# Transposes moved from TensorE to the DMA queue, and copies between ScalarE and VectorE, in a linear-attention and MLP kernel

## The chip, the cores and the metric

The kernel runs on one core of one Trainium2 chip. A core has TensorE (matmuls), VectorE, ScalarE and GpSimd (work element by element), SyncE (here it only issues DMA transfers) and 16 DMA engines. The metric is the device time of one launch in microseconds (us), the median of several launches; lower is better. A profile is taken from one launch more. Its span, first to last instruction, is somewhat shorter than the launch. In profiles PE is TensorE, DVE is VectorE, ACT is ScalarE, POOL is GpSimd, and SP or SPq is SyncE with its DMA queue.

## The reference, cut to what matters

Two parts follow each other: a recurrent attention over 768 steps for 4 batches and 8 heads of width 48, and an MLP with a squared relu on its output.

```python
# r, k, v, w: (4, 8, 768, 48); u: (8, 48); w_in: (384, 2048); w_out: (2048, 384)
for t in range(S):
    cur = np.einsum('bhd,bhe->bhde', u[None] * kt, vt)
    y[:, :, t] = np.einsum('bhd,bhde->bhe', rt, state + cur)
    state = wt[:, :, :, None] * state + np.einsum('bhd,bhe->bhde', kt, vt)
x = y.transpose(0, 2, 1, 3).reshape(3072, 384)
h = x @ w_in
g = s * np.maximum(h, 0.0) ** 2 + b
out = g @ w_out                               # (3072, 384), float32
```

## The kernel before

The 768 steps are cut into 6 chunks of 128, so there are 24 chunk-batches, numbered n = 0 to 23. For each of them the kernel loads w, r, k and v (`load n.0` to `load n.3`), takes logarithms and cumulative sums of w (`ln`, `cum`, `exp`, and from n = 8 on `inc` and `exn`), scales r and k with them (`mul`, tile `prd`), transposes both (`tr` with its copy `tev`), multiplies them (`mt`), masks (`msk`), forms the output y (`ymm`, `yev`, tile `x_sb`), transposes that (`xtr` with its copy `xev`) into `xT`, and updates the state (`dmm`, `sup`, `st`). Two chunk-batches make one MLP tile T of 256 tokens. Each of the 12 MLP tiles has eight pieces of the first product (`g1T.i`, 6 matmuls each), their relu (`reluT.i`) and square (`sqT.i`), and eight pieces of the second (`g2T.i`, 4 matmuls each; tile 11 has 12, eight of them of half width), then `oev` and `store`. `li`/`ci` and `lo`/`co` load and cast the four parts of the two weights.

The transposes come in two forms, chosen by the number of the chunk-batch:

```python
def xbar_rk(n):
    return n >= DTK or (n >= DK2 and n % 2 == 1)     # DTK = 9
def xbar_x(n):
    return n >= DTX or (n >= DX2 and n % 2 == 1)     # DTX = 24: never

def trans(n):                       # "tr" on TensorE: 8 matmuls into PSUM
    for x in range(2):
        for p in range(HP):
            nc.tensor.matmul(ps[:, x * HP + p, :], lhsT=..., rhs=identity, is_transpose=True, ...)
def tevac(n):                       # "tev" on ScalarE: PSUM to SBUF
    nc.scalar.copy(out=RK, in_=c["trps"])
def dtrans(n):                      # "tev" as one transposing DMA instead of both
    nc.sync.dma_start_transpose(out=RK, in_=c["prd"].rearrange("t x h d -> t (x h d)"))

def xtr(n):                         # "xtr" on TensorE: 3 matmuls into PSUM
    for i in range(KT):
        nc.tensor.matmul(ps[:, i, :], lhsT=c["x"][:, i*128:(i+1)*128], rhs=identity, is_transpose=True, ...)
def xevac(n):                       # "xev" on ScalarE
    nc.scalar.copy(out=xT[T][:, :, j * L : (j + 1) * L], in_=c["xt_ps"])
def dxtr(n):                        # "xev" as one transposing DMA
    nc.sync.dma_start_transpose(out=xT[T][:, :, j * L : (j + 1) * L], in_=cb[n]["x"])
```

The MLP, with two PSUM buffers for `h_ps`:

```python
def g1(T, i):
    ps = psH.tile([128, FPQ, TOK], FP32, name="h_ps", tag="h")        # 2 buffers
    for f in range(FPQ):              # 2
        for kt in range(KT):          # 3
            nc.tensor.matmul(ps[:, f, :], lhsT=w_in_sb..., rhs=xT[T][:, kt, :], ...)
def relu(T, i):
    rh = mlp.tile([128, FPQ, TOK], BF16, name="rh", tag="rh", bufs=4)
    nc.scalar.activation(out=rh, in_=hs[T, i], func=AF.Relu)
def square(T, i):                     # on ScalarE or VectorE, by the order's text
    ...
def warm(n):                          # n matmuls on zeros, into a tile that nobody reads
    for _ in range(n):
        nc.tensor.matmul(warm_ps, lhsT=warm_sb[:, 0:128], rhs=warm_sb, start=True, stop=True)
```

The order in which instructions are issued isn't left to a scheduler. It is a text of words that an earlier search found, and each engine runs its own words in that order. A word such as `g10.4` is piece 4 of `g1` of MLP tile 0; `+5` is a call of `warm(5)`; a suffix `@A` or `@D` puts the word on ScalarE or VectorE in place of its default engine.

Of the kernel before, what the change touches and what calls it, by code (L numbers as in the profile page):

```python
# [24 lines left out]
PK = 2  # L25
PKD = 1.55
ONE = 8
DTK = 9
DTX = 24
DK2 = 24  # L30
DX2 = 24
SQE = 'DA'
# [15 lines left out]
g11.3 load6.0 colsum1 rkp4 g20.1 ln5 relu1.2 tr4 rku4 relu1.3 load4.3 cum5 sq1.0@A g11.4 st1 exp5
g11.5 co2 g20.5 tev4 load5.1 sq1.3 load5.2 colsum2 sq1.1@A st3 co3 mt4 load7.0 relu1.4 g20.6
relu1.5 cd4 g11.6 load6.1 msk4 sq1.5@A colsum3 ln6 g20.7 yd4 sq1.4@A load6.2 cssplit g11.7 sq1.2@A  # L50
l25 l24 vb4@A csspread load5.3 cum6 csevac g20.2 mul5 exp6 load8.0 dmm4 g20.3 rkp5 sup4 ln7
load6.3 tr5 oev0.0 ymm4 rku5 tev5 cum7 load7.1 yev4 g21.0 oev0.1 exp7 l26 xtr4 mul6 load7.2 g21.1
xev4 mt5 relu1.6 cd5 vb5 load7.3 g21.4 relu1.7 st2 msk5 yd5 dmm5 g21.2 ln8 load9.0 sq1.7@A st4
sup5 tr6 cum8 vb6 store0.1 tev6 ymm5 rkp6 g21.5 yev5 exp8 load8.1 g21.6 inc8 l27 sq1.6@A dmm6 xtr5
mul7 g21.7 load8.3 xev5 exn8 mt6 rkp7 sup6 vb7@A load8.2 g12.0 msk6 load9.1 g12.1 rku7 ln9 tr7
oev1.1 relu2.0 load10.0 rku6 cum9 relu2.1 cd7 dmm7 g12.2 inc9 tev7 l28 load11.0 g12.3 cd6 st5
relu2.2 ymm6 yd6 sup7 load9.2 exp9 g12.4 relu2.3 sq2.0 mt7 yd7 yev6 exn9 load9.3 g12.5 relu2.4
msk7 st7 g21.3 sq2.2@A store0.0 sq2.1 rkp8 g12.6 oev1.0 sq2.3 load10.1 ymm7 relu2.6 st6 xtr6 g22.4
yev7 ln10 load10.2 mul8 relu2.5 g22.0 ln11 xtr7 sq2.4 load12.0 g22.5 xev6 sq2.6@A load10.3 cum10
# [24 lines left out]
inc19 exp19 load19.1 g16.7 mul18 load19.2 g17.0 relu6.7 tev16 g26.1 exn19 ln20 dmm16 g26.5 vb18@A
sup16 load19.3 sq6.7 cum20 g17.1 vb17 inc20 relu7.0 tev17 g26.6 rkp18 sq6.6@A dmm17 relu7.1 g17.2
st16 exp20 load20.1 dmm18 g26.7 sq7.0@A mul19 exn20 g26.2 tev18 relu7.2 rkp17 oev6.1 g17.3 sup17
mt16 rku17 relu7.3 load20.2 g17.4 msk16 sq7.3 g26.3 yd16 relu7.4 load21.0 g17.5 sup18 sq7.2@A vb19
cd17 sq7.1 ymm16 rku18 tev19 oev6.0 mt17 relu7.5 g27.0 msk17 l219 yd17 g27.4 st17 load21.1 g17.6
yev16 ymm17 st18 load21.2 xtr16 mt18 yev17 xev16 g27.5 sq7.5@D relu7.6 load22.0 sq7.4 xtr17 cd18
g17.7 xev17 mul20 ln21 g27.1 relu7.7 dmm19 load20.3 yd18 msk18 g18.0 sq7.7 sq7.6@A g27.2 rkp19  # L90
store5.1 sup19 relu8.0 g27.6 rku19 mt19 tev20 g18.1 msk19 rkp21 ymm18 relu8.1 g18.2 load23.0 sq8.0
g27.3 store6.1 rku21 cd19 relu8.2 load22.1 cum21 ln22 g18.3 sq8.1@D exp21 ymm19 yd19 inc21 relu8.3
g18.4 oev7.0 sq8.2@A rkp20 g27.7 load22.2 yev19 relu8.4 yev18 g18.5 sq8.3 rku20 oev7.1 load23.1
mt20 relu8.5 load21.3 xtr18 xtr19 msk20 vb20@A g18.6 xev18 g28.0 load22.3 relu8.6 supn20 sq8.5@D
g18.7 sq8.4 xev19 store6.0 exn21 cum22 g19.0 relu8.7 inc22 rkp22 ln23 g28.1 load23.2 relu9.0 g28.4
mul21 sq8.6@A store7.0 g19.1 exp22 supn21 cd20 exn22 g28.5 tev21 yd20 relu9.1 cum23 ymm20 exp23
g19.2 yev20 g28.6 inc23 relu9.2 mul22 g19.3 sq8.7 exn23 g28.2 tev22 sq9.1 mul23 g19.4 sq9.2@A
xtr20 relu9.3 cd21 g28.3 load23.3 sq9.0 sq9.3 g28.7 yd21 oev8.0 relu9.4 store7.1 g19.5 store8.0
rku22 mt21 relu9.5 g19.6 vb22 msk21 sq9.5 st19 g29.4 vb21@A tev23 xev20 g19.7 oev8.1 relu9.6
supn22 cd22 ymm21 sq9.4@A g29.5 yd22 yev21 relu9.7 mt22 sq9.6@A vb23 g29.0 sq9.7@D xtr21 rkp23  # L100
msk22 g29.6 xev21 g29.1 rku23 g110.0 ymm22 relu10.0 g110.1 yev22 mt23 cd23 relu10.1 g110.2 yd23
msk23 xtr22 g29.7 relu10.2 supn23 sq10.0@A g110.3 xev22 ymm23 relu10.3 g110.4 yev23 g29.2 sq10.1@D
relu10.4 g110.5 sq10.3 sq10.4 oev9.1 xtr23 g110.6 relu10.5 sq10.2 xev23 g210.0 sq10.5@D relu10.6
g110.7 g111.0 relu10.7 g210.1 relu11.0 g111.1 g210.2 relu11.1 g111.2 sq11.0@A sq10.6@A g29.3
sq10.7 g111.3 oev9.0 relu11.2 g210.3 sq11.1@D relu11.3 store9.0 store8.1 g111.4 sq11.2@A g210.4
relu11.4 g111.5 g210.5 relu11.5 g111.6 sq11.5@D oev10.0 g210.6 relu11.6 sq11.3@D store10.0 g111.7
store9.1 g211.0 relu11.7 g210.7 sq11.4@A sq11.7@D sq11.6@A g211.1 oev10.1 g211.4 store10.1 g211.2
g211.8 g211.5 g211.3 g211.6 oev11.0 g211.9 g211.7 store11.0 g211.10 oev11.1 g211.11 store11.1
oev11.2 store11.2
"""  # L110

class Plan:

# [43 lines left out]
def kernel(  # L160
# [550 lines left out]
        T, j = divmod(n, CPT)  # L711
        if j == 0:
            xT[T] = mlp.tile([128, KT, TOK], BF16, name="xT", tag="xT", bufs=XTB)
        nc.scalar.copy(out=xT[T][:, :, j * L : (j + 1) * L], in_=c["xt_ps"])  # L714


    def load_win(i):
# [40 lines left out]

    def relu(T, i):
        rh = mlp.tile([128, FPQ, TOK], BF16, name="rh", tag="rh", bufs=4)  # L760
        nc.scalar.activation(out=rh, in_=hs[T, i], func=AF.Relu)  # L761
        hs[T, i] = rh

    def sq_eng(T, i):
# [385 lines left out]
```

## Time and profile before

| what | before |
|---|---|
| device time, median of 3 (lowest to highest) | 187.79 us (187.76 to 187.91) |
| span of the profile | 186.2 us |
| TensorE: busy, matmuls | 180.6 us, 1994 |
| VectorE busy | 131.5 us |
| ScalarE busy | 142.4 us |
| GpSimd busy | 103.8 us |
| transposing DMAs, median time to landing | 15, 3.3 us |
| mean granted TensorE clock | 0.999 of full speed |

Busy time counts a matmul from its start to its modelled end. Matmuls overlap, so the busy time can exceed the time they take from the queue: where this document speaks of a **slot** it means the time from the start of one group of matmuls to the start of the next group on TensorE. The chain of waits is followed back from the last instruction, each step to what released it. The timeline lists instructions in order of time.

### The profile page before, as it was taken

How to read it: one execution, taken by the hardware profiler on the slowest of the kernel's cores; microseconds unless marked ns; L12 is line 12 of the kernel's file. 1: busy time of each engine (PE TensorE's matmuls, PEld its weight loads, DVE VectorE, ACT ScalarE, POOL GpSimd, SP SyncE). 2: the span in 40 equal slices, each digit the busy share in tenths (PEclk: the TensorE clock that was granted, in tenths of full speed). 3: DMA queues.
4: the chain of work that ended last, by engine and by line, in shares of the span. 5: the costliest groups of instructions: out<-in, count | busy, mean ns of one | idle time of the engine just before them, and what ended most of it. 6: DMA issues, size and time to landing. Idle time of an engine off the chain costs nothing.

```text
span 186.2 us, 5073 instructions
## 1 busy us (share of the span) xinstructions
PE 180.6 (97%) x1994; PEld 142.3 (76%) x1994; DVE 131.5 (71%) x220; ACT 142.4 (76%) x277; POOL 103.8 (56%) x141
## 2 busy tenths in 40 slices
PE   7999999999999999999999999999999999999992
PEld 5667888866678788687778877877787877887871
DVE  7478888556799768986987878658788577452231
ACT  3576798797979999769798779974689886678530
POOL 3787840608798695949956265695892167100000
PEclk9999999999999999999999999999999999999999
DMA  6998999888989999999488989999698272000322
GB/s 161 264 308 239 331 318 280 295 180 177 207 190 229 197 221 240 187 213 188 118 199 171 246 164 252 194 186 208 146 212 211 59 184 59 2 0 4 112 99 86
DMA packets 117610, 34.14 MB, mean 183 GB/s; under 512 B 112338, under 2 KB 115539, under 8 KB 117587
## 3 DMA queue, kind: packets, MB, share of 16 engines
q1 hardware_dynamic: 117586, 33.83, 78.3%
q8 instruction: 15, 0.25, 0.5%
q14 instruction: 9, 0.07, 0.1%
HBM read 25.17 MB, written 4.72 MB: 160 GB/s over the span
## 4 chain that ended last, share of the span: by engine, by line
PE 74%; SPq 12%; DMA 7%; DVE 4%; issue 1%; DVEq 0%
PE o_ps L792 31%; PE h_ps L748 29%; SPq L297 8%; DMA wi_st<-in_moe_w_in_dram 5%; PE mt_ps L543 3%; DMA rkt<-in_k_dram 2%; PE y_ps L606 2%; PE xt_ps L699 2%; PE y_ps L597 2%; PE cums L388 2%; PE d_ps L638 1%; DVE gT L773 1%; SPq L719 1%; SPq L305 1%; PE trps L477 1%; SPq L729 1%
## 5 line engine op out<-in xcount | busy, mean ns | idle before, releaser
L748 PE MATMUL h_ps<-xT,w_in 128*128 128x256 bf16 x576 | 77.6, 273 | 0.1
L792 PE MATMUL o_ps<-w_out,gT 128*128 128x384 bf16 (+1 forms) x400 | 75.3, 320 | 0.0
L761 ACT ACTIVATE rh<-h_ps 128x512 bf16<-128x512 f32 x96 | 56.5, 598 | 14.5 <-PE h_ps L748 13.5
L748 PEld LDWEIGHTS <-w_in 128*128 128x128 bf16 x576 | 60.6, 114 | 6.7 <-POOL w_in L880 0.2
L792 PEld LDWEIGHTS <-gT 128*128 128x128 bf16 x400 | 36.2, 98 | 15.3
L771 ACT ACTIVATE gT<-rh 128x512 bf16<-128x512 bf16 x62 | 37.2, 629 | 0.3
L352 POOL TENSOR_TENSOR yd<-vt,cd 128x384 bf16<-128x384 f32 x22 | 20.1, 919 | 30.4 <-DVE cd L346 18.3
L554 DVE TENSOR_TENSOR mt_sb<-mt_ps,tri_strict 128x1024 bf16<-128x1024 f32 x22 | 26.8, 1219 | 4.2 <-PE mt_ps L543 3.8
L323 POOL TENSOR_TENSOR rkp<-rkt 128x384 f32<-128x384 f32 x22 | 24.5, 1112 | 4.7 <-DMA rkt<-in_k_dram 4.6
L329 POOL TENSOR_TENSOR rku<-rkp,u_bc 128x384 f32<-128x384 f32 x24 | 26.0, 1087 | 0.9
L451 DVE TENSOR_TENSOR prd<-rkt,E 128x768 bf16<-128x768 f32 x22 | 23.0, 1045 | 2.8 <-DMA rkt<-in_k_dram 1.6
L803 DVE SCALAR_TENSOR_TENSOR o_sb<-o_ps,s_bc,bconst 128x384 f32<-128x384 f32 (+1 forms) x25 | 14.9, 596 | 10.3 <-PE o_ps L792 10.0
L651 DVE TENSOR_TENSOR x_sb<-y_ps,yd 128x384 bf16<-128x384 f32 x24 | 13.2, 554 | 11.3 <-PE y_ps L606 10.4
L773 DVE TENSOR_TENSOR gT<-rh 128x512 bf16<-128x512 bf16 x34 | 15.8, 482 | 4.9 <-ACT rh L761 4.9
L714 ACT COPY xT<-xt_ps 128x384 bf16<-128x384 bf16 x24 | 11.5, 478 | 6.8 <-PE xt_ps L699 6.8
L346 DVE TENSOR_REDUCE cd<-rku 128x8 f32<-128x384 f32 x24 | 13.0, 543 | 0.9 <-POOL rku L329 0.9
L688 POOL TENSOR_TENSOR st<-stmp,l 128x384 bf16<-128x384 bf16 x16 | 13.1, 829 | 0.7 <-DVE stmp L679 0.7
L1109 PE MATMUL warm_ps<-warm_sb 128*128 128x256 bf16 x74 | 12.2, 309 | 1.1 <-DVE warm_sb L1066 1.1
L424 DVE TENSOR_TENSOR inc<-cums,logw 128x384 f32<-128x384 f32 x16 | 8.9, 554 | 5.5 <-ACT rh L761 1.6
L318 ACT ACTIVATE logw<-wt 128x384 bf16<-128x384 f32 x22 | 11.5, 522 | 1.5 <-DMA wt<-in_w_dram 1.3
L880 POOL CAST vb<-vt 128x384 bf16<-128x384 f32 x14 | 7.4, 536 | 7.6 <-DMA vt<-in_v_dram 4.9
L464 POOL TENSOR_TENSOR l<-E,par 128x8 f32<-128x8 f32 x20 | 7.0, 353 | 6.6 <-ACT E L419 4.7
(96 smaller groups left out, 198.1 us busy)
## 6 DMA issues: line engine op xcount, KB each, us to landing
out_dram<-o_sb SPq DMA_DIRECT2D x23, 192.0 KB, 2.8
wt<-in_w_dram SPq DMA_DIRECT2D x22, 192.0 KB, 3.9
rkt<-in_r_dram SPq DMA_DIRECT2D x22, 192.0 KB, 4.0
rkt<-in_k_dram SPq DMA_DIRECT2D x22, 192.0 KB, 3.8
vt<-in_v_dram SPq DMA_DIRECT2D x22, 192.0 KB, 3.7
wi_st<-in_moe_w_in_dram SPq DMA_DIRECT2D x4, 768.0 KB, 7.5
wo_st<-in_moe_w_out_dram SPq DMA_DIRECT2D x4, 768.0 KB, 7.6
pkt<-in_w_dram SPq DMA_DIRECT2D x1, 384.0 KB, 3.3
```

The costliest lines, as they stand in the source:

```text
L297: nc.sync.dma_start(out=dst, in_=src[bb, :, t0 : t0 + L, :].transpose([1, 0, 2]))
L323: nc.gpsimd.tensor_tensor(out=rkp, in0=c["r"], in1=c["k"], op=ALU.mult)
L329: nc.gpsimd.tensor_tensor(out=rku.rearrange("t h d -> t (h d)"), in0=c["rkp"].rearrange("t h d -> t (h d)"), in1=u_bc, op=ALU.mult,)
L352: nc.gpsimd.tensor_tensor(out=yd, in0=c["v"], in1=c["cd"].unsqueeze(2).to_broadcast([128, H, D]), op=ALU.mult,)
L451: nc.vector.tensor_tensor(out=prd[:, :, :, 0:D], in0=c["rk"], in1=c["E"][:, :, 0:HD].rearrange("t x (h d) -> t x h d", h=H), op=ALU.mult,)
L554: nc.vector.tensor_tensor(out=m.rearrange("s g p t -> s (g p) t"), in0=c["mt_ps"].rearrange("s g p t -> s (g p) t"), in1=(masks[n % 2] if ...
L748: nc.tensor.matmul(ps[:, f, :], lhsT=w_in_sb[ft // FPP][:, kt, :].rearrange("p (m j) -> p j m", j=FPP)[:, ft % FPP, :], rhs=xT[T][:, kt, : ...
L761: nc.scalar.activation(out=rh, in_=hs[T, i], func=AF.Relu)
L771: nc.scalar.activation(out=g, in_=rh, func=AF.Square)
L773: nc.vector.tensor_tensor(out=g, in0=rh, in1=rh, op=ALU.mult)
L792: nc.tensor.matmul(os_[T, k][:, cols], lhsT=gT[T][:, ft, tt * 128 : (tt + 1) * 128], rhs=w_out_sb[ft // FPP][:, ft % FPP, cols], start=(ft ...
L803: nc.vector.scalar_tensor_tensor(out=o_sb[:, cols], in0=os_.pop((T, k))[:, cols], scalar=s_bc, in1=bconst[:, cols], op0=ALU.mult, op1=ALU.add,
```

## The change

One chunk-batch more (n = 8) has its r and k transposed by a DMA, and the last four (n = 20 to 23) have x transposed by a DMA; before, no x was. That takes these transposes off TensorE and their copies off ScalarE. The copy of x out of PSUM and the relu can now run on VectorE too, where the order's text says so, which is meant to share the work between ScalarE and VectorE more evenly. The order's text is new from end to end, since it was searched again for the new choices. It has 80 warm-up matmuls where the old one had 74. By its suffixes and defaults the new text puts 26 of 96 relus and 10 of the 20 remaining copies of x on VectorE; the squares on ScalarE go from 62 to 63, the casts of v there from 10 to 11, one cast of `w_out` moves from VectorE to ScalarE, and one cast of `w_in` from VectorE to GpSimd.

```diff
@@ -25,8 +25,8 @@
 PK = 2
 PKD = 1.55
 ONE = 8
-DTK = 9
-DTX = 24
+DTK = 8
+DTX = 20
 DK2 = 24
 DX2 = 24
...
@@ the order of issue @@
 ORDER = """
-load0.0 load0.1 load_u load0.2 load2.0 ln0 ln1 load2.1 +18 cum0 load2.2 u_mm exp0 load0.3 +2 cum1
-l20 mul0 li0 exp1 rkp1 u_ev +1 tr0 load3.1 ln2 mul1 tev0 load3.2 +6 cum2 rku1 +2 tr1 exp2 load2.3
-l21 tev1 mul2 vb0@A l22 cd1 +14 mt0 rkp2 vb1@A msk0 +5 dmm0 load3.0 rkp0 tr2 sup0 +1 mt1 tev2 li1
-rku0 st0 msk1 ci0 load3.3 rku2 cd0 +13 mt2 li2 ymm0 yd0 msk2 vb2@A yd1 +1 ymm1 li3 yev0 rkp3 ln3
-xtr0 yev1 xev0 +3 cum3 cd2 rku3 dmm2 xtr1 exp3 load4.0 sup2 +6 dmm1 xev1 mul3 lo0 ci1@A +2 ymm2
-g10.0 l23 cd3 yd2 sup1 g10.1 relu0.0 vb3 yev2 tr3 relu0.1 small2 yd3 g10.2 tev3 dmm3 ci2@D g10.3
-relu0.2 xtr2 sup3 mt3 sq0.0@A load4.1 g10.4 sq0.1 relu0.3 msk3 ci3 g10.5 relu0.4 lo1 xev2 ymm3 ln4
-sq0.2 relu0.5 g10.6 sq0.3 load4.2 yev3 cum4 relu0.6 load5.0 xtr3 g10.7 co0 xev3 lo2 g11.0 relu0.7
-sq0.4 sq0.5 g20.0 relu1.0 sq0.6 sq0.7 colsum0 exp4 lo3 g11.1 g11.2 co1 relu1.1 small g20.4 mul4
-g11.3 load6.0 colsum1 rkp4 g20.1 ln5 relu1.2 tr4 rku4 relu1.3 load4.3 cum5 sq1.0@A g11.4 st1 exp5
-g11.5 co2 g20.5 tev4 load5.1 sq1.3 load5.2 colsum2 sq1.1@A st3 co3 mt4 load7.0 relu1.4 g20.6
-relu1.5 cd4 g11.6 load6.1 msk4 sq1.5@A colsum3 ln6 g20.7 yd4 sq1.4@A load6.2 cssplit g11.7 sq1.2@A
-l25 l24 vb4@A csspread load5.3 cum6 csevac g20.2 mul5 exp6 load8.0 dmm4 g20.3 rkp5 sup4 ln7
-load6.3 tr5 oev0.0 ymm4 rku5 tev5 cum7 load7.1 yev4 g21.0 oev0.1 exp7 l26 xtr4 mul6 load7.2 g21.1
-xev4 mt5 relu1.6 cd5 vb5 load7.3 g21.4 relu1.7 st2 msk5 yd5 dmm5 g21.2 ln8 load9.0 sq1.7@A st4
-[... cut: 50 lines ...]
-msk22 g29.6 xev21 g29.1 rku23 g110.0 ymm22 relu10.0 g110.1 yev22 mt23 cd23 relu10.1 g110.2 yd23
-msk23 xtr22 g29.7 relu10.2 supn23 sq10.0@A g110.3 xev22 ymm23 relu10.3 g110.4 yev23 g29.2 sq10.1@D
-relu10.4 g110.5 sq10.3 sq10.4 oev9.1 xtr23 g110.6 relu10.5 sq10.2 xev23 g210.0 sq10.5@D relu10.6
-g110.7 g111.0 relu10.7 g210.1 relu11.0 g111.1 g210.2 relu11.1 g111.2 sq11.0@A sq10.6@A g29.3
-sq10.7 g111.3 oev9.0 relu11.2 g210.3 sq11.1@D relu11.3 store9.0 store8.1 g111.4 sq11.2@A g210.4
-relu11.4 g111.5 g210.5 relu11.5 g111.6 sq11.5@D oev10.0 g210.6 relu11.6 sq11.3@D store10.0 g111.7
+load0.0 load_u load0.2 load0.1 load2.0 load2.1 ln0 +18 u_mm ln1 load2.2 +1 cum0 exp0 load0.3 +5
+cum1 mul0 load3.0 rkp0 exp1 +1 tr0 load2.3 ln2 mul1 tev0 li0 +6 cum2 l20 u_ev +2 tr1 exp2 rku0
+load3.1 tev1 mul2 load3.2 vb0@A +15 mt0 vb1 cd0 tr2 ln3 msk0 rkp1 load3.3 dmm0 tev2 l21 sup0 l22
++7 mt1 rku1 st0 dmm1 msk1 li1 yd0 sup1 +10 cum3 rkp2 load4.0 cd1 ymm0 exp3 yd1 lo0 +1 ymm1 ci0
+yev0 l23 rkp3 li2 mt2 yev1 xtr0 mul3 +2 xtr1 xev0 vb2@A rku2 xev1@D vb3@A +7 tr3 li3 msk2 g10.0
+tev3 dmm3 ci1 load5.0 sup3 +5 mt3 relu0.0@D dmm2 g10.1 sup2 rku3 sq0.0@A g10.2 cd2 relu0.1 load4.1
+msk3 ymm2 yd2 relu0.2 g10.3 ln4 co0 sq0.1@A ymm3 load4.2 yev2 g20.0 cd3 xtr2 ci2 g20.4 sq0.2 yd3
+cum4 lo1 yev3 exp4 g10.4 relu0.3@D ci3 xtr3 small2 xev2@D g10.5 sq0.3@A relu0.4@D ln5 colsum0 lo2
+relu0.5@D sq0.4@A g10.6 xev3@D g10.7 lo3 relu0.6 sq0.5 cum5 relu0.7 mul4 g11.0 sq0.6@A g11.1 rkp4
+relu1.0 load4.3 tr4 relu1.1 load6.0 g11.2 co1 tev4 g11.3 sq0.7 load5.1 exp5 g20.1 relu1.2@D
+colsum1 relu1.3 co2 g11.4 sq1.0@A g20.5 l25 rku4 small relu1.4@D g11.5 co3@A load5.2 mt4 cd4 g20.2
+sq1.4 vb4 load7.0 colsum2 yd4 colsum3 g20.6 cssplit ln6 load6.1 msk4 l24 csspread dmm4 load6.2
+g20.7 csevac sq1.1 load5.3 sq1.3@A g11.6 sq1.2@A mul5 cum6 load8.0 relu1.5 g20.3 exp6 rkp5 sup4
+tr5 load6.3 oev0.0 g11.7 ln7 rku5 relu1.6@D tev5 ymm4 load7.1 oev0.1 cum7 relu1.7 g21.4 yev4
+load7.2 exp7 mul6 xtr4 g21.0 load9.0 vb5 st2 cd5 mt5 st4 xev4@D st1 tr6 ln8 st3 msk5 g21.5 load7.3
+rkp6 tev6 dmm5 g21.1 sup5 load8.3 sq1.5@A l26 cum8 yd5 ymm5 inc8 exp8 g21.6 load8.1 rku6 vb6@A
+[... cut: 44 lines ...]
+ln23 g28.0 oev7.1 sq8.4@A tev21 g28.1 inc22 sq8.6@A g28.4 cd20 exn22 xev19@D yd20 cum23 load21.3
+g28.5 inc23 exp23 store7.1 g19.0 supn21 sq8.7@D mt20 rkp22 relu9.0@D load23.2 g28.6 msk20 st18
+g19.1 g19.2 load23.3 mul22 ymm20 relu9.2 g28.2 store6.1 relu9.1 sq9.2 mt21 yev20 tev22 sq9.1 g28.7
+vb21 msk21 sq9.0@A yd21 g19.3 exn23 xev20 g19.4 relu9.3 mul23 g28.3 sq9.3 load22.3 relu9.4 ymm21
+vb23 oev8.0 g19.5 sq9.4@A tev23 st19 yev21 g19.6 oev8.1 relu9.5 rkp23 g29.0 sq9.5 relu9.6@D
+store7.0 g29.1 rku22 supn22 g29.2 sq9.6 xev21 g19.7 rku23 cd22 mt22 relu9.7 g29.4 yd22 store8.0
+msk22 g29.5 vb22 g29.6 sq9.7@D mt23 ymm22 g29.7 yev22 g110.0 cd23 xev22 msk23 yd23 g29.3 relu10.0
+g110.1 sq10.0@A oev9.0 g110.2 relu10.1 supn23 store9.0 ymm23 sq10.1@D relu10.2 g110.3 yev23
+sq10.2@A g210.0 relu10.3@D g110.4 oev9.1 xev23 g110.5 sq10.3@D relu10.4@D g210.4 relu10.5 store8.1
+g210.5 sq10.4@A store9.1 sq10.5@D g210.1 g110.6 g110.7 relu10.6@D g210.2 relu10.7 g111.0 sq10.6@A
+g111.1 relu11.0@D g210.6 sq11.0 relu11.1 sq10.7@D g111.2 sq11.1@D g111.3 relu11.2@D g210.3
+relu11.3 g111.4 sq11.3@D oev10.0 g111.5 relu11.4@D store10.0 g211.0 relu11.5 sq11.2 g111.6 sq11.5
...
@@ -711,7 +712,11 @@
         T, j = divmod(n, CPT)
         if j == 0:
             xT[T] = mlp.tile([128, KT, TOK], BF16, name="xT", tag="xT", bufs=XTB)
-        nc.scalar.copy(out=xT[T][:, :, j * L : (j + 1) * L], in_=c["xt_ps"])
+        out = xT[T][:, :, j * L : (j + 1) * L]
+        if pl.ops["xev", n]["eng"] == "ACT":
+            nc.scalar.copy(out=out, in_=c["xt_ps"])
+        else:
+            nc.vector.tensor_copy(out=out, in_=c["xt_ps"])
 
 
     def load_win(i):
@@ -758,7 +763,10 @@
 
     def relu(T, i):
         rh = mlp.tile([128, FPQ, TOK], BF16, name="rh", tag="rh", bufs=4)
-        nc.scalar.activation(out=rh, in_=hs[T, i], func=AF.Relu)
+        if pl.ops["relu", T, i]["eng"] == "ACT":
+            nc.scalar.activation(out=rh, in_=hs[T, i], func=AF.Relu)
+        else:
+            nc.vector.tensor_scalar_max(out=rh, in0=hs[T, i], scalar1=0.0)
         hs[T, i] = rh
 
     def sq_eng(T, i):
```

## The prediction

> **What bounds the kernel now.** I read the page first (busy times), then the chain of waits in order of time, then busy time by stage, then TensorE's timeline.
>
> The page has TensorE busy all the time:
>
> ```profile
> span 186.2 us, 5073 instructions
> PE 180.6 (97%) x1994; PEld 142.3 (76%) x1994; DVE 131.5 (71%) x220; ACT 142.4 (76%) x277; POOL 103.8 (56%) x141
> L748 PE MATMUL h_ps<-xT,w_in 128*128 128x256 bf16 x576 | 77.6, 273 | 0.1
> L761 ACT ACTIVATE rh<-h_ps 128x512 bf16<-128x512 f32 x96 | 56.5, 598 | 14.5 <-PE h_ps L748 13.5
> ```
>
> The first row after the span is busy time, the next two are groups: busy time, mean ns of one, idle time before them with what ended it. The 97% alone shows little, as one `h_ps` matmul lasts 273 ns but the six of a piece take 0.65 us of the queue, 109 ns each. The chain of waits (start, duration, what) shows where TensorE really sets the pace:
>
> ```profile
> 39.27 4.35 DMA rkt<-in_k_dram
> 43.74 0.97 DVE prd L451
> 44.76 0.62 PE trps L477 x8
> 45.99 0.67 PE o_ps L792 x4
> 63.91 0.45 PE trps L477 x8
> 172.11 0.65 PE h_ps L748 x6
> 176.68 5.90 PE o_ps L792 x52
> 182.60 0.42 DVE o_sb L803
> ```
>
> Up to 44.76 us the chain passes through transfers: the last is the k of chunk-batch 5 (`load5.2`), which releases `mul5` (tile `prd`) and with it the eight transposes `tr5`. After that the chain has only TensorE rows in all its longer steps, until the last matmul ends at 182.6. Is there slack inside these rows? I added up slots, from TensorE's timeline: 0.65 us a `g1` or `g2` piece (0.33 half width), 0.45 a `tr`, 0.165 an `xtr`, 0.33 an `mt`, 0.38 a `ymm` with a state (0.21 without, 0.98 in the packed n = 0, 1), 0.17 a `dmm` (0.45 packed), 0.95, 0.43, 0.26 and 0.16 the four kinds of `cum`, and 0.31, 0.49 and 0.84 for `colsum`, `csspread` and `u_mm`. All that stands behind `tr5` in the order of before comes to 134.8 us. It took 182.6 - 44.8 = 137.8. The 3 us between are mostly rounding of the slots and the change of tile shape after an `mt`; I found no single hole over 0.2 us. Hence **TensorE bounds the kernel from 45 us on, with nearly no wait in it**, and transfers bound the head. Busy time by stage agrees (stretch, its length, then PE, PEld, DVE, ACT, POOL busy, the clock, the DMA share and GB/s):
>
> ```profile
> 22.00:44.70 22.70, 22.02 (x259) 18.04 (x254) 15.59 (x27) 19.30 (x37) 9.03 (x12) 1.00 0.92 259
> 44.70:80.00 35.30, 35.24 (x407) 27.48 (x408) 30.43 (x47) 31.07 (x62) 28.35 (x36) 1.00 1.04 210
> 80.00:120.00 40.00, 40.00 (x435) 32.24 (x434) 31.52 (x50) 35.07 (x73) 25.42 (x35) 1.00 0.92 195
> 120.00:163.00 43.00, 43.00 (x462) 33.90 (x460) 30.66 (x49) 32.53 (x66) 25.39 (x29) 1.00 0.66 141
> 163.00:182.60 19.60, 19.57 (x162) 15.73 (x159) 6.77 (x15) 11.01 (x21) 0.00 (x0) 1.00 0.15 54
> ```
>
> ScalarE is at 88% between 45 and 120 us, close behind but not the bound; the DMA engines are full until 120 and nearly idle at the end.
>
> **What the Trainium skill says.** (1) "Perfetto Trace Analysis", Identifying the Most-Contended Engine: matmul busy time is no measure of how near TensorE is to its limit, since matmuls overlap. The trace agrees (273 ns busy, 109 ns of queue), so I count slots. (2) "VectorE: DVE Perf Modes", The three transpose paths: 390 ns on TensorE and 1309 ns by DMA for one 128x128 block. Here a block costs TensorE only 56 ns of queue (eight in 0.45 us), and eight blocks by DMA land 3.3 us after issue. (3) "ScalarE: Activation LUTs", What ACT_TABLE_LOAD costs: 186 ns + 0.833 ns an element, 612 ns for a relu of 512; the trace has 598. (4) "VectorE: DVE Perf Modes", Why PSUM operands drop a tier: float32 from PSUM runs at one element a cycle, and two at most otherwise. The trace has no single-source float32 op of 512 from PSUM, but two-source ones: 554 ns for 384 elements (`x_sb`) and 1219 for 1024 (`mt_sb`), 1.04 ns an element.
>
> **The change part by part.**
>
> 1. *r and k of n = 8 by DMA.* Removed: `tr8`, eight matmuls, the row at 63.91 us, 0.45 us, in a stretch where TensorE has no hole. Also a copy of 1.01 us on ScalarE. Added: a transposing DMA of some 3.3 us to landing, at about 62 to 65 us, where the DMA share is 1.04. So **-0.45 us**, if `mt8` stands far enough behind. In the new order, where `tev8` is issued just behind `xtr7`, four `g1` and four `g2` pieces, two `cum` and two `dmm` stand between `xtr7` and `mt8`: 8 x 0.65 + 2 x 0.26 + 2 x 0.17 = 6.1 us.
> 2. *x of n = 20 to 23 by DMA.* Removed: 4 x 0.165 = 0.66 us of TensorE and four copies of 0.48 us on ScalarE, between 147 and 165 us. Added: four DMAs where the share is 0.66 falling to 0.15. From `ymm21` to `g110.0` ten pieces of 0.65 us stand in the new order, and ten between `ymm23` and `g111.0`: 6.5 us each, against about 0.55 (`yev`) + 3.3 (landing, as an estimate from the larger transpose). Hidden: **-0.66 us**.
> 3. *Warm-ups.* Six more, at the 0.11 us that one takes in the filled queue: +0.66 us of TensorE, five of them just behind `dmm3` in tile 0's `g1`. They are padding for a wait that the search expected there.
> 4. *Relu and copies of x on VectorE.* Relu on VectorE, estimated from the two rows above: 554 + 128 x 1.04 = 0.69 us, 26 of them 17.9 us; ten copies at 0.35 to 0.55, 3.5 to 5.5; less one square (0.48) and two casts (0.96 each). VectorE goes from 131.5 to about 151 us. ScalarE loses 26 x 0.598 + 14 x 0.478 + 1.01 = 23.2 us and gains a square (0.63), a cast of v (0.51) and one of w_out (1.5, as `w_in`'s 1486 ns): about 122 us. As TensorE had no wait on ScalarE behind 45 us that would show, this frees **nothing by itself**.
> 5. *The new order.* I compared what stands ahead of `tr5`, the first instruction of the saturated part. The loads ahead of `load5.2` are the same set in both orders. TensorE's words ahead of `tr5` are the same too, but for six more warm-ups (+0.66) and `g11.7` moved behind it (-0.65): 38.71 us of slots before, 38.72 after. So `tr5` should start at about 44.8 again. Behind it stand 134.8 + 0.65 - 0.45 - 0.66 = 134.3 us of slots, **0.46 us less**.
>
> Sum: the DMA fixes the head, the removed transposes are worth 1.11 us, the warm-ups eat 0.66 of it. 187.79 - 0.46 = 187.33. As a new order was searched for and kept, I take a little off for holes that it may have closed in the head: **187.2 us**.
>
> **Rivals.** (a) *The head gets faster:* warm-ups in the queue cost nothing if TensorE would have waited anyway, and `tr5` may come earlier, by a better order of transfers. For it: the chain of before passes through the queue of transfers from 15 to 44 us. Against it: the same bytes stand ahead of `load5.2`, and the share is already 0.92. It would give the full 1.1 us or somewhat more: 186.0 to 186.7. (b) *VectorE becomes the bound:* the new text puts ten VectorE relus in tiles 0 to 2, and a late relu holds one of only two `h_ps` buffers. For it: VectorE is at 86% between 45 and 80 us already (30.43 of 35.3). Against it: in tiles 3 to 8 only seven relus move. TensorE would get holes of some tenths each, 1 to 3 us in all: 188 to 190. (c) *The head gets slower:* `load4.0` and `lo0` now stand ahead of `li2`, 0.96 MB at about 260 GB/s, 3.7 us later, and `g10.4` needs it. The new order has `g20.0`, `g20.4` and the warm-ups ahead of `g10.4` to fill that, some 1.9 us. What isn't filled is lost only if it is still there at `tr5`: up to +1 us. (d) *A transposing DMA delays loads* around 65 us by its few us: loads run ahead by several chunk-batches there, so I give it little.
>
> **Range and chances.** (a) sets the low end, (b) and (c) the high end: 186.1 to 188.9. Two per cent are 3.8 us, more than any of the rivals but a bad (b) could make. Faster by over 2%: 0.02, within: 0.94, slower: 0.04.
>
> **What would show it.** TensorE has 1980 matmuls (1994 - 20 + 6); `trps` has 64 and `xt_ps` 60. `tr5` starts near 44.8 us (step 5; earlier speaks for (a), later for (c)). From there to the last matmul it is about 137.4 us (steps 1, 2); more means holes, with `h_ps` matmuls waiting for VectorE (b). ScalarE busy is near 122, VectorE near 151, one relu on VectorE near 0.69 us (step 4). The prediction fails if the new order's holes in the head differ from the old one's by more than a microsecond, which I can't read from an order alone.

## The result, and the profile after

The changed kernel takes **189.92 us** (median of 4 runs, 189.5 to 191.04) against 187.77 us for the kernel before in the same comparison: a ratio of **1.0129, 95% interval 1.0081 to 1.0177**. It is 2.15 us slower where 187.2 us and a small gain were predicted, and it lies above the predicted range.

The profiled execution is the one of 191.04 us, so its times run about 1 us above the median. Its page, with the span, the busy times and the group of the new relus (busy time, mean ns of one | idle time before it and what ended it):

```profile
span 189.1 us, 5050 instructions
PE 182.1 (96%) x1980; PEld 142.2 (75%) x1980; DVE 152.5 (81%) x253; ACT 126.0 (67%) x239; POOL 106.2 (56%) x141
...
L769 DVE TENSOR_SCALAR rh<-h_ps 128x512 bf16<-128x512 f32 x26 | 17.8, 683 | 6.2 <-PE h_ps L753 5.9
```

The balance of work came out as meant: fewer matmuls, ScalarE relieved of 16 us, 21 us more on VectorE. TensorE is still at 96%. Neither row shows a loss. The chain of waits does (start, duration, what):

```profile
22.24 1.38 DVE prd L452
...
28.36 0.58 DVE w_out L890
...
31.76 0.69 DVE rh L769
32.50 0.81 PE h_ps L753 x6
...
46.98 0.72 DVE prd L452
47.75 0.62 PE trps L478 x8
...
54.02 0.57 DVE inc L425
54.67 0.50 ACT E L420
55.21 0.40 PE mt_ps L544 x8
```

Two things differ from before. `tr5`, the row at 47.75 us, is **3.0 us later** (44.76 before). And the chain ahead of it no longer runs through transfers: from 22 to 32 us it runs mostly through VectorE, with the new relu (31.76 us) in it, and from 32.5 us on mostly through TensorE, but for 2.8 us on ScalarE (36.8 to 39.6 us) and the product `prd` just ahead of `tr5`. Behind `tr5` it still leaves TensorE now and then, as at 54.02 us, where `mt` waits for an `exp` behind an `inc` on VectorE. The last matmul ends at 185.9, 138.2 us after `tr5`; it was 137.8 before.

**A ledger of lost time.** With the slots of the prediction I added up TensorE's useful work ahead of a mark, by each kernel's own text and without warm-ups, and took it from the time at which the mark starts. What is left is lost time: waits, warm-ups, and matmuls at a lower rate. Unlike the bare times of marks, it lets orders be compared that have done different work by then. In us:

| stretch | before | after | difference |
|---|---|---|---|
| start, to the first `g1` piece (21.95; 24.12) | 12.44 | 14.54 | +2.10 |
| middle, from there to `tr4` (34.91; 36.57) | 0.67 | 2.06 | +1.39 |
| `tr4` to `tr5` (44.76; 47.75) | 1.08 | 1.23 | +0.15 |
| `tr5` to the last matmul's end (182.56; 185.93) | 3.02 | 3.86 | +0.84 |
| useful work removed | | | -1.11 |
| sum | | | +3.37 |

The text does have 1.11 us less work in it. The changed order adds four times as much lost time, most of it ahead of `tr4`, where the prediction had counted only the warm-ups.

### The profile page after: what moved, and what is told of

It reads as the page before. It is cut to its first block, busy times and chain, and to the rows that moved or that the text cites. A ratio compares the mean times of both kernels' runs of the same rounds, so it can differ in the third digit from the quotient of the medians.

```text
span 189.1 us, 5050 instructions
## 1 busy us (share of the span) xinstructions
PE 182.1 (96%) x1980; PEld 142.2 (75%) x1980; DVE 152.5 (81%) x253; ACT 126.0 (67%) x239; POOL 106.2 (56%) x141
## 4 chain that ended last, share of the span: by engine, by line
PE 80%; DVE 7%; issue 2%; ACT 2%; POOL 1%; DVEq 0%; ACTq 0%
PE h_ps L753 30%; PE o_ps L800 30%; PE mt_ps L544 4%; PE warm_ps L1117 2%; PE y_ps L607 2%; DVE prd L452 2%; PE cums L389 2%; PE y_ps L598 2%; PE trps L478 2%; PE xt_ps L700 2%; PE d_ps L639 1%; DVE rh L769 1%; DVE inc L425 1%; ACT E L420 1%; PE y_ps L587 1%
## 5 line engine op out<-in xcount | busy, mean ns | idle before, releaser
L753 PE MATMUL h_ps<-xT,w_in 128*128 128x256 bf16 x576 | 74.1, 273 | 0.4 <-DVE rh L769 0.2
L767 ACT ACTIVATE rh<-h_ps 128x512 bf16<-128x512 f32 x70 | 41.2, 596 | 25.2 <-PE h_ps L753 24.4
L779 ACT ACTIVATE gT<-rh 128x512 bf16<-128x512 bf16 x63 | 38.1, 627 | 1.6 <-DVE rh L769 1.1
L452 DVE TENSOR_TENSOR prd<-rkt,E 128x768 bf16<-128x768 f32 x22 | 27.8, 1265 | 1.4 <-ACT E L435 0.8
L769 DVE TENSOR_SCALAR rh<-h_ps 128x512 bf16<-128x512 f32 x26 | 17.8, 683 | 6.2 <-PE h_ps L753 5.9
L781 DVE TENSOR_TENSOR gT<-rh 128x512 bf16<-128x512 bf16 x33 | 17.7, 543 | 1.8 <-ACT rh L767 1.7
L652 DVE TENSOR_TENSOR x_sb<-y_ps,yd 128x384 bf16<-128x384 f32 x24 | 13.2, 550 | 4.9 <-PE y_ps L607 2.8
L689 POOL TENSOR_TENSOR st<-stmp,l 128x384 bf16<-128x384 bf16 x16 | 14.1, 884 | 5.4 <-DVE stmp L680 5.4
L1117 PE MATMUL warm_ps<-warm_sb 128*128 128x256 bf16 x80 | 13.4, 316 | 1.1 <-DVE warm_sb L1074 1.1
L420 ACT ACTIVATE E<-cums 128x388 f32<-128x388 f32 (+1 forms) x16 | 7.9, 493 | 8.3 <-DVE inc L425 5.9
L347 DVE TENSOR_REDUCE cd<-rku 128x8 f32<-128x384 f32 x24 | 12.9, 539 | 0.0
L413 ACT ACTIVATE E<-cums 128x768 f32<-128x768 f32 x8 | 6.5, 817 | 8.6 <-PE cums L381 4.7
```

Of the source, the lines that this page charges most:

```text
L452: nc.vector.tensor_tensor(out=prd[:, :, :, 0:D], in0=c["rk"], in1=c["E"][:, :, 0:HD].rearrange("t x (h d) -> t x h d", h=H), op=ALU.mult,)
L753: nc.tensor.matmul(ps[:, f, :], lhsT=w_in_sb[ft // FPP][:, kt, :].rearrange("p (m j) -> p j m", j=FPP)[:, ft % FPP, :], rhs=xT[T][:, kt, : ...
L769: nc.vector.tensor_scalar_max(out=rh, in0=hs[T, i], scalar1=0.0)
L779: nc.scalar.activation(out=g, in_=rh, func=AF.Square)
L781: nc.vector.tensor_tensor(out=g, in0=rh, in1=rh, op=ALU.mult)
```

## The experiments

Theory A blamed one word: `u_mm` (two float32 matmuls of one row for u) now stands ahead of `cum0` and delays the start. Rivals were VectorE as the bound (B), GpSimd holding VectorE up, and the order of transfers or of words as a whole. Below, ratios are to the kernel before, with 95% intervals; medians are over all executions, while ratios leave out those that ran in a slower state of the chip.

**1. `u_mm` back behind `cum0`, in the changed kernel** (`e1_after_u_late`).

```diff
-+18 u_mm ln1 load2.2 +1 cum0 exp0
++18 ln1 load2.2 +1 cum0 u_mm exp0
```

> The changed kernel, with the spread of u (u_mm, two float32 matmuls) issued behind cum0 instead of ahead of it, as in the kernel before. Theory A (u_mm stands ahead of cum0 while TensorE is still cold, and the head of the whole attention chain shifts by it): cum0 starts near 4.9 us instead of 6.8, g10.0 near 22 instead of 24.1, time 187.7 to 188.2, about 2 us less than the changed kernel's 189.9. Rival B (VectorE is the bound, by relus and copies): within 0.4 us of 189.9. Rival C (the transposing DMAs cost it): within 0.4 us of 189.9.

Measured: 190.94 us, 1.0163 [1.0104, 1.0222]. The first `g1` piece does start 1.5 us earlier (22.61 us), but `tr5` only 0.8 (46.98). The waits of TensorE from 20 to 50 us (in all, times, longest) show one that took its place, for the last cast of w_out:

```profile
PE cs_ps L839 <- ACT w_out L886: 1.5, 1, 1.5
PE o_ps L800 <- DVE w_out L890: 0.5, 1, 0.5
...
```

The kernel is no faster than the changed one (189.92 us, 1.0129): in time, the whole of the earlier start is lost again. As the whole cause, A falls.

**2. The same word moved early, in the kernel before** (`e2_before_u_early`): `+18 cum0 load2.2 u_mm` becomes `+18 u_mm cum0 load2.2`.

> The kernel before, with u_mm moved ahead of cum0 and nothing else. Theory A: cum0 starts near 6.7 us, g10.0 near 24, time 189.3 to 190.0, about 2 us more than before's 187.8. Rivals B and C: 187.8, as nothing of VectorE or of the transposes changes.

Measured: 188.98 us, 1.0097 [1.0059, 1.0134]. In an order that is otherwise unchanged the word costs 1.4 us, or 1.8 by the ratio. `cum0` starts at 6.42 us where it was at 4.87. So an early `u_mm` is harmful in this order, and in the changed one taking it away is not enough.

**3. The transposes alone, in the kernel before** (`e3_before_crossbar`): `DTK = 8`, `DTX = 20`, without `tr8` and `xtr20` to `xtr23`.

> The kernel before in its own order, with only the transposes of the change: r and k of n=8 and x of n=20 to 23 by DMA, their TensorE words left out of the order. Theory A, and the step of the prediction that values the removed transposes at 1.11 us: 186.5 to 187.0. Rival C (DMA transposes stall the order): 188 or more, with TensorE holes near 65 us or behind 147 us.

Measured: 186.95 us, 0.9973 [0.9949, 0.9997]. It is a gain, of about half the 1.11 us of slots (the interval reaches from 0.1 to 1.0 us). A wait that may have eaten the rest, from 60 to 75 us:

```profile
PE mt_ps L543 <- DMA RK<-prd: 1.1, 1, 1.1
```

In the old order the transfer has too little in front of `mt8`; the changed order has more, and its `mt8` doesn't wait for the transfer. With `DTX = 20` alone (`e10_before_x_only`):

> The kernel before with only x of n=20 to 23 by DMA; r and k of n=8 stay on TensorE. With both by DMA in before's order, mt8 waited 1.14 us for its transposing DMA, which takes back more than the 0.45 us of tr8. So without that: 0.66 us less than before, 186.7 to 187.0, and not slower than with both.

Measured: 188.23 us, 1.001 [0.9979, 1.0041]: no gain outside the interval, with one wait of 0.4 us for a transposed x. Without the wait of `mt8` it should have been the faster of the two, and it was not. So whether these four are worth their 0.66 us, and whether that wait is what halved the gain of experiment 3, stays open.

**4. All relus and copies of x on ScalarE, in the changed kernel** (`e4_after_scalar`): the `@D` of 26 relus and 10 `xev` is taken off.

> The changed kernel with all 26 relus and 10 copies of x on ScalarE again. Theory A: still 189 to 190.5, as the late head stays; VectorE busy near 131, ScalarE near 145. Rival B (VectorE is what slows it): 187.5 to 188.5, and the mean of the prd products back from 1265 to about 1050 ns.

Measured: 192.71 us, 1.0265 [1.0221, 1.0309]. Sharing with VectorE **helps**, by about 2.5 us (from the two ratios to before). It helps behind `tr5` (140.6 us to the end in place of 138.2), and changes little ahead of it (`tr5` at 47.39 us).

**5. The two orders joined at `tr5`.** `e5_head_before` has the order of before up to `tr5`, then the changed one; `e6_head_after` is its mirror image, with before's transposes. Each word of the second part that the first has issued already is left out.

> The changed kernel with the order of before up to tr5 (74 warm-ups, u_mm behind cum0, all relus and copies of x there on ScalarE) and its own order behind it. tr5 should then start near 44.9 us, as in the kernel before. Theory H (the loss is made in the head, by the order of transfers, the cold TensorE and warm-ups): 187.0 to 187.8, with 137.4 to 138 us from tr5 to the last matmul. Theory S (the stretch from 45 to 75 us, where VectorE and ScalarE hold each other up, makes it too): 188.3 to 189.2, with 139 or more from tr5 to the end.

> The kernel before with the changed order up to tr5 (80 warm-ups, u_mm ahead of cum0, relus and copies of x partly on VectorE), and its own order and transposes behind it. Theory H: tr5 near 47.4 us, 189.7 to 190.7. Theory S: no more than about 188.5, since the new order's stretch behind tr5 is absent.

Measured: 187.51 us, 0.9999 [0.9978, 1.0019], and 191.01 us, 1.021 [1.016, 1.0261]. The loss goes with the head. Yet the first has 1.11 us less work and gains nothing by it, so the changed order behind `tr5` is no better either.

**6. More of the head repaired.** `e7_u_late_loads` is experiment 1 with before's sequence of loads up to `load5.2`. `e9_u_late_wout_early` is experiment 1 with the last three parts of w_out loaded earlier and `co3` on VectorE.

> The changed kernel with u_mm behind cum0 and, on the transfer queue, the loads up to load5.2 in the order of before (li0 two loads earlier, li2 and li3 ahead of load4.0 and lo0). Theory H in its form that the order of transfers sets tr5: tr5 near 45 us, 187.8 to 188.6. If the order of transfers doesn't matter and VectorE's own order in the head does: tr5 near 47, as with u_mm late alone, and about 190.5.

> The changed kernel with three repairs of its head: u_mm behind cum0; lo1 ahead of load4.2 and load5.0, and lo2, lo3 before small2, so that the parts of w_out land earlier; the cast co3 on VectorE (0.96 us) in place of ScalarE (1.48). lo0 stays early. If the head's waits are what is left of the loss once u_mm is late (with u_mm late alone colsum3 waited 1.46 us for that cast, and nothing was gained): no wait of TensorE on w_out over 0.5 us, tr5 near 45.5 us, time 188.0 to 189.0. If something else holds the head: tr5 at 47 or later and 190 or more.

Measured: 191.64 us, 1.0223 [1.0171, 1.0275], and 190.74 us, 1.0181 [1.0142, 1.022]. In `e7` TensorE waits for the first w_out part:

```profile
PE o_ps L799 <- DVE w_out L889: 2.4, 1, 2.4
```

The new words have `g20.0` early and need `lo0` early; before's loads bring it late. Behind that wait TensorE's matmuls ran at half rate for a while, as the last section shows. In `e9` the wait of experiment 1 is gone, and smaller ones stand in its place:

```profile
PE trps L477 <- DVE prd L451: 0.7, 2, 0.6
PE o_ps L799 <- DVE w_out L889: 0.5, 1, 0.5
PE h_ps L752 <- ACT rh L766: 0.4, 1, 0.4
...
```

**7. GpSimd's products on one head of eight**, in both kernels (`e12_after_gpsimd_cut`, `e13_before_gpsimd_cut`). Most of the product of r, k and u is left out, so the outputs differ from the reference.

> The changed kernel, with GpSimd's products r*k and r*k*u on one head of eight only (the rest of the diagonal term is left out, the sum on VectorE reads the same number of elements); so its output isn't the reference's. Theory L (VectorE's products of two float32 tiles in SBUF, tile prd, are held up while GpSimd runs its own): the mean of the prd products falls from 1265 to about 950 ns, mul5 no longer takes 1.75 us, and the time falls by 0.8 to 2 us from 189.9. If the hold-ups lie off the path: prd faster all the same, and the time within 0.5 us.

> The same cut of GpSimd's two products in the kernel before, as the other half of the comparison. The mean of prd falls from 1045 to about 950 ns. Theory L (hold-ups on VectorE make the new order slower): the gain here is small, under 0.4 us, so that the distance of the two kernels shrinks from 2.1 us to about 1. If the distance stays at 2 us, they don't explain it.

Measured: 189.72 us, 1.011 [1.0068, 1.0151], and 187.44 us, 0.9987 [0.9959, 1.0016]. VectorE's `prd` of 768 elements does get faster, from a median of 1.24 us in the changed kernel to 0.95, which is the median of before. The distance of the kernels stays at 2.3 us. In the profile of the changed kernel so cut, TensorE's waits for `prd` are gone, but another one stands in the head:

```profile
PE cs_ps L841 <- ACT w_out L888: 1.4, 1, 1.4
```

Behind it, too, matmuls ran at half rate. Being held up beside GpSimd is real; by itself it is not the cause.

**8. The head cut into three.** `f1_before_to_tr3` and `f2_before_to_tr4` take before's order to `tr3` or `tr4` and the changed order from there; `f3_after_to_tr3` and `f4_after_to_tr4` are their mirror images.

> The order of before up to tr3 (about 23 us; without the transposes that DTK = 8 and DTX = 20 do away with), then the changed order for all that is left. If the loss arises in the start, ahead of tr3 (u_mm and the cold TensorE among it), this is at before's time: 187.2 to 188.2, tr5 at 44.5 to 45.5. If it arises in the stretch between tr3 and tr5 (first MLP pieces of tile 0 and 1, w_out parts, relu on VectorE), it is 189.0 to 190.3 with tr5 at 46.5 to 47.5.

> The order of before up to tr4 (about 35 us), then the changed order. If the loss arises in the start: at before's time, 187.2 to 188.0. If in the middle: at before's time as well, if it lies between tr3 and tr4, but 188.5 to 190 if it lies between tr4 and tr5 (w_out's last part, mul5 beside GpSimd).

> The mirror image: the changed order up to tr3, then the order of before, with before's transposes. If the loss arises in the start: 189.5 to 191, tr5 at 46.8 or later. If in the middle: 187.5 to 188.7, since TensorE catches up on what the start left (it is waiting for transfers anyhow), tr5 at 45 to 45.8.

> The changed order up to tr4 (about 36.6 us), then the order of before with before's transposes. If the loss lies ahead of tr4: 189.5 to 191. If between tr4 and tr5: 187.8 to 189.

Measured, in this sequence: 190.16 us, 1.0168 [1.011, 1.0226]; 188.11, 1.0046 [1.0019, 1.0072]; 190.76, 1.0195 [1.0148, 1.0242]; 192.03, 1.027 [1.0227, 1.0314]. Either part alone, the new start or the new middle, gives a slow kernel; only `f2`, which has neither, is near before. The waits of TensorE from 20 to 50 us, first `f1`, then `f3`:

```profile
PE o_ps L799 <- DVE w_out L889: 1.8, 1, 1.8
PE h_ps L752 <- ACT rh L766: 0.7, 1, 0.7
...
```

```profile
PE h_ps L747 <- DVE w_in L881: 1.8, 1, 1.8
PE y_ps L605 <- DVE mt_sb L553: 1.6, 2, 1.1
```

A part of one order needs weights at times at which the loads of the other don't bring them. So these four do not add up like terms: a joint makes waits of its own, and the reading "start alone" or "middle alone" is not clean.

**9. Before's engines in the changed head.** Between 22 and 36 us VectorE is nearly full in the changed kernel. Busy time in that stretch (its length, then PE, PEld, DVE, ACT, POOL, the clock, the DMA share, GB/s), first before, then after:

```profile
22.00:36.00 14.00, 13.87 (x169) 12.19 (x165) 10.85 (x19) 11.94 (x22) 6.95 (x8) 1.00 0.98 305
```

```profile
22.00:36.00 14.00, 13.02 (x153) 10.74 (x154) 12.95 (x22) 10.30 (x18) 8.03 (x7) 1.00 0.94 306
```

That is 12.95 of 14 us, where it was 10.85. `g1_after_engines_before` gives twenty words of the head (relus and squares of MLP tiles 0 and 1, copies of x, casts of v) the engines of before; `g2_u_late_engines_before` also has `u_mm` late.

> The changed kernel with the engines of before for the relus and squares of MLP tiles 0 and 1, the copies of x of chunk-batches 1 to 3 and the casts of v of 0 to 5 (twenty words in the head; the order itself stays). VectorE is busy 11.45 of 12.5 us between the first g1 piece and tr4 in the changed kernel, 10.6 of 12.95 before. If that load on VectorE is what costs the middle of the head, this is at 188.0 to 189.0 us, and TensorE loses 0.6 to 1.1 us between the first g1 piece and tr4 in place of 2.1. If it is the order of words and transfers, not the engine, it stays at 189.4 to 190.8, or ScalarE becomes the one to wait for.

> The same twenty engines of before, and u_mm behind cum0 as well. If the two together are the cause (TensorE cold in the start, VectorE full in the middle), this is near before's time or below: 187.2 to 188.2, with tr5 at 45 to 45.6. If the cause is in the order of words and transfers, 189.5 to 191, tr5 at 46.7 or later, with a wait for the last cast of w_out as when u_mm alone was moved.

Measured: 190.32 us, 1.0116 [1.0073, 1.016], and 189.66 us, 1.0116 [1.0074, 1.0157]. The middle loses 2.7 us in both, not less than in the changed kernel, now with 0.7 us of waits for relus on ScalarE. The chain passes through the load on VectorE, but moving that load to ScalarE mends nothing. Nor did `u_mm` matter between these two: their ratios are the same.

**10. The best of both** (`e8_before_to_g14`): the order of before as far as `g14.0`, with `DTK = 8` and without `tr8`, then the changed order with `DTX = 20`.

> The changed kernel with the order of before up to g14.0 (about 95 us; tr8 is left out there and r, k of n=8 go by DMA), and its own order behind it. Theory S: 187.0 to 187.6, that is 1 to 1.5 us less than with before's order only up to tr5. Theory H: the same as with before's order up to tr5, within 0.4 us.

Measured: **187.10 us, 0.9971 [0.9952, 0.999]**. Its median is below both kernels', and it is faster than before by half a microsecond. Experiment 3 does about as well.

**The ledger over the runs.** Lost time in us by stretch, from one profile each, as in the table above:

| kernel | start | middle | `tr4` to `tr5` | behind |
|---|---|---|---|---|
| before | 12.44 | 0.67 | 1.08 | 3.02 |
| before, `u_mm` early (2) | 13.88 | 1.01 | -0.07 | 3.06 |
| before, transposes (3) | 12.61 | 1.39 | 0.40 | 4.22 |
| before to `tr5` (5) | 13.04 | 0.46 | -0.04 | 4.84 |
| before to `g14.0` (10) | 13.06 | 0.46 | -0.07 | 4.43 |
| before to `tr4` (8) | 12.55 | 1.09 | 1.16 | 4.16 |
| before to `tr3` (8) | 12.62 | 4.12 | 0.15 | 3.87 |
| after | 14.54 | 2.06 | 1.23 | 3.86 |
| after, `u_mm` late (1) | 13.03 | 2.06 | 1.97 | 4.13 |
| the same, w_out early (6) | 13.14 | 3.03 | 0.68 | 3.88 |
| the same, loads of before (6) | 13.15 | 5.18 | -0.05 | 3.84 |
| after, all on ScalarE (4) | 13.28 | 3.36 | 0.83 | 6.24 |
| after, engines of before (9) | 12.65 | 2.72 | 0.70 | 3.68 |
| after to `tr5` (5) | 15.63 | 3.36 | 0.26 | 3.06 |
| after to `tr3` (8) | 13.63 | 3.24 | -0.07 | 3.12 |
| after to `tr4` (8) | 15.67 | 3.55 | -0.08 | 3.06 |

Small negative numbers are rounding of the slots. The column of the middle divides the kernels: 0.5 to 1.4 us with the words of before in start and middle, 2.1 to 5.2 in all others, whatever engines, loads or start they have. (In the 5.2, that of `e7`, are the wait of 2.4 us and the half rate behind it.)

## Why the prediction was wrong

**The step that failed is step 5**, "So `tr5` should start at about 44.8 again". Its sums hold: the same loads and 38.7 us of slots stand ahead of `tr5` in both texts. But useful slots ahead of `tr5` are only some 30 us of that; the rest of its 44.8 us was 14.2 us of lost time (warm-ups, at 0.11 us each, fill 8.1 of them), and that is a property of the order. In the changed order it is 17.8 us. The prediction said that it fails if the heads' holes differ by more than a microsecond, and still centred on zero; its range gave the head too little.

The other half of the step, that the last of the equal loads sets `tr5`, failed as well. Three rows of the changed kernel's timeline, with others between them left out (POOL here starts when the k of chunk-batch 5 has landed; what ended the idle time ahead of a row stands at its end):

```profile
44.73 1.00 POOL L324 TENSOR_TENSOR rkp<-rkt 128x384 f32<-128x384 f32 x1 [1.89 <-DMA rkt<-in_k_dram]
45.94 1.75 DVE L452 TENSOR_TENSOR prd<-rkt,E 128x768 bf16<-128x768 f32 x1
47.75 0.62 PE L478 MATMUL trps<-identity,prd 128*128 128x128 bf16 x8 [0.81 <-DVE prd L452]
```

In the kernel before, `mul5` began as soon as the same k landed, at 43.74 us, and took 0.97. So the 3.0 us are 1.0 of a later landing, 1.2 in which VectorE was still busy with other words, and 0.8 of a longer product (GpSimd ran its own at the same time in both). Yet none of these alone would bring `tr5` back, since TensorE's own words ahead of it ended only at 46.9. The landing goes with the order: between 42.0 and 43.9 us in the eight profiles with before's order up to `tr4` or further, between 44.5 and 46.2 in the nine with the changed order and its loads from `tr3` to `tr4`. But `e7`, with before's loads, had this k by 43.0 and still started `tr5` only at 48.2.

- *Start, +2.1 us.* In four kernels with the changed start and `u_mm` late the start loses 12.9 to 13.2 us, near what before's start does (12.2 to 13.1 in eight profiles). With `u_mm` early it loses 12.6 to 15.7 in seven. So this part goes with `u_mm` and the rate of the matmuls around it, which the last section shows, and the profile of after happens to lie in the upper half of that spread; the medians may hold less of it. Nor did a late `u_mm` make the changed kernel faster (experiments 1 and 9): other waits took the gain. No step of the prediction looked at where `u_mm` stands.
- *Middle, +1.4 us.* 0.55 us are the five warm-ups of step 3. They are padding, as that step said: `mt3`, the next word, needs ScalarE's copy of `tr3`, which ends at 25.33 us, and its weight load waits for it even so (three rows, others between them left out):

```profile
24.32 1.01 ACT L501 COPY RK<-trps 128x1024 bf16<-128x1024 bf16 x1 [0.73 <-PE trps L478]
24.95 0.71 PE L1117 MATMUL warm_ps<-warm_sb 128*128 128x256 bf16 x5
25.58 0.23 PEld L544 LDWEIGHTS <-RK 48*128 48x128 bf16 x8 [0.21 <-ACT RK L501]
```

  So taking the warm-ups away should gain little, which no run tried. The loss is in the order: between `tr3` and `mt3` that of before has two `g1` pieces, a `dmm` and an `xtr`, the changed one only one `g1` piece and a `dmm`. The other 0.8 are small holes, such as these two of TensorE's timeline:

```profile
29.36 0.81 PE L800 MATMUL o_ps<-w_out,gT 128*128 128x384 bf16 x4 [0.49 <-DVE w_out L890]
...
32.50 0.70 PE L753 MATMUL h_ps<-xT,w_in 128*128 128x256 bf16 x5 [0.25 <-DVE rh L769]
```

  Why this middle can't be mended by one change is shown only so far: not by `u_mm`, the loads, w_out's transfers, the engines of its words, or GpSimd. Each repair opened another wait. That it is the fit of words and transfers is what is left; a single cause was not found.
- *Behind `tr5`: 138.2 us where 137.4 was predicted.* Steps 1 and 2 removed what they said. Two waits took it back, with slots 0.42 and 0.63 us too long, 1.05 in all. (Of each, 0.1 us stands ahead of nearly every `mt`, in the kernel before too, and is most of what the prediction put down to rounding and tile shape. So 0.85 are new.)

```profile
55.21 0.40 PE L544 MATMUL mt_ps<-RK 48*128 48x128 bf16 x8 [0.26 <-ACT E L420]
...
73.77 0.40 PE L544 MATMUL mt_ps<-RK 48*128 48x128 bf16 x8 [0.46 <-ACT E L420]
```

  They stand in the changed order behind `tr5` whatever the head is (`e5` and `f2` have 1.0 and 1.1 us of the same wait), and not in before's. The tile of `mt` and the sums of `cum` share one PSUM buffer in the kernel's text, so `mt` comes behind the `inc` and `exp` that read the sums. The first row is `mt6`, two of TensorE's words behind `cum8`. VectorE had been idle for 0.4 us ahead of that `inc`, waiting for `cum8`, so the words stand too close. The second is `mt8`, the word for which step 1 had counted 6.1 us of room for the transfer. The transfer was in time, but VectorE came to `inc12` only at 72.58 us, some 1.4 us behind its sums, after this product:

```profile
70.91 1.75 DVE L452 TENSOR_TENSOR prd<-rkt,E 128x768 bf16<-128x768 f32 x1
```

  With GpSimd's products cut (experiment 7) this second wait is gone, and the stretch takes 137.6 us.
- *Steps 1 and 2 by themselves* were worth about 0.5 us in the old order (experiment 3), half of the sum. There the time to landing was not covered; whether that is all that is missing stays open (`e10`).
- *Step 4* was right in its sizes (relu 0.683 us for 0.69, VectorE 152.5 for 151), and 126 on ScalarE for 122: the durations of ScalarE's groups do add up to some 20 us less than before, but consecutive instructions overlap, and its busy time fell by only 16.4. Its sentence that moving the relus "frees nothing by itself" holds for the old order; in the changed one, taking them back cost about 2.5 us (experiment 4).
- *Rivals.* (a) didn't happen. (b) had its own case, a late relu that holds one of two `h_ps` buffers, once, at 32.50 us, for 0.25 us; VectorE was late ahead of `tr5` and `mt8` too, but by products and not by relus. (c) had the direction, a slower head, but not the reason: no wait for `w_in` is among TensorE's waits in the changed kernel. Nor did (d) show: behind `tr5` its only waits for others over 0.2 us are those two.

The ledger explains the two profiles, 3.4 us apart; the medians are 2.15 apart, as the profiled execution of the changed kernel is its slowest of four.

## What to carry to other kernels

Equal sets of loads and equal work ahead of a mark don't fix when it is reached: where an engine waits or pads, the lost time is the larger unknown, and a new order of issue has to be given a range as wide as a good part of it. Lost time per stretch, useful slots taken from the time of a mark, found a loss here that busy shares and the chain hid. And a new order could not be mended here word by word, as each repair opened another wait. The old order with only the removed instructions left out (experiment 3) gained 0.5 us, where the new one lost 2.

## What the runs showed of the hardware

The same words at the start did not take the same time. TensorE's timeline from 5 to 8 us, in the changed kernel and then in `g1`, whose text is the same as far as there (start, duration, what):

```profile
5.00 1.64 PE L909 MATMUL u_ps<-u_row,one_row 1*128 1x384 f32 x2
...
6.77 0.84 PE L374 MATMUL cums<-logw,hs_pos 128*128 128x384 bf16 x2
...
8.48 1.25 PE L1117 MATMUL warm_ps<-warm_sb 128*128 128x256 bf16 x5
```

```profile
4.77 0.91 PE L907 MATMUL u_ps<-u_row,one_row 1*128 1x384 f32 x2
...
5.72 0.49 PE L372 MATMUL cums<-logw,hs_pos 128*128 128x384 bf16 x2
...
6.75 0.72 PE L1115 MATMUL warm_ps<-warm_sb 128*128 128x256 bf16 x5
```

In the first, matmuls run at half rate until about 9.8 us, in the second at full rate from 4.8 us on, and the profile's clock row shows full speed in both. The Trainium skill, "TensorE: Matmul & The Clock Gate", What's actually happening, says that TensorE starts at half its clock and goes to full speed after a window of some 3.4 us with enough activity, and that this window runs freely, so that the moment varies from run to run. The traces agree in the factor of two. The moment scatters more here than the half a microsecond that the section gives, from about 4.8 to 9.8 us in these two. What they add is what this costs: with `u_mm` straight behind the 18 warm-ups, `xtr0` started between 20.0 and 23.0 us in seven profiles; with the changed start and `u_mm` behind `cum0`, between 20.3 and 20.5 in four. That matmuls of a single row count as too little activity would explain it; it was not measured by itself.

Half rate came back behind waits, in two runs. In `e7` TensorE waited 2.4 us until 29.89 us; the same form of matmul then and later:

```profile
31.78 0.52 PE L388 MATMUL cums<-logw,tri_strict 128*128 128x384 bf16 x1
...
36.55 0.33 PE L388 MATMUL cums<-logw,tri_strict 128*128 128x384 bf16 x1
```

The next matmul followed 0.32 us behind the first and 0.17 behind the second. In `e12` it was so behind a wait of 1.4 us: from 45.04 us the four matmuls of a `g2` piece took 1.19 us in place of 0.65. So each of these waits cost some 1.6 us more than its length, by an estimate from the slots. Behind the waits of 1.5 us in `e1` and 1.8 us in `f1` and `f3` no such stretch shows; what decides was not measured.
